# A fused GLA and gated-SSM kernel: the third turn's order, two loads of the second, and the place of an If

## The chip, the cores and the metric

The kernel runs on one core of a Trainium2 chip. The metric is the device time of one execution in microseconds (us). The engines are named as in the profile: PE is TensorE (PEld its weight loads), DVE is VectorE, ACT is ScalarE, POOL is GpSimd, SP is SyncE, which here issues most of the DMAs. Each engine runs its own instructions in the program's order, and engines wait for one another through semaphores.

## The reference

Two layers follow one another. The first is gated linear attention: a state for each of 8 heads decays by alpha and takes in an outer product at each of 768 steps. The second projects the result to a value and a gate, runs a decaying sum over the values, multiplies by the gate's SiLU and projects back. All data are float32 (the weights arrive as float64).

```python
# q, k, v, alpha: (B=4, H=8, S=768, D=48)
for t in range(S):
    state = alpha[:, :, t, :, None] * state + np.einsum('bhd,bhe->bhde', k[:, :, t], v[:, :, t])
    y[:, :, t] = np.einsum('bhd,bhde->bhe', q[:, :, t], state)
x = y.transpose(0, 2, 1, 3).reshape(B, S, H * D)        # (4, 768, 384)
proj = x @ w_in                                         # (4, 768, 1024)
val, gate = proj[..., :512], proj[..., 512:]
a = np.exp(A_log)
for t in range(S):
    h = a * h + val[:, t, :]
    ys[:, t, :] = h
out = (gate * sigmoid(gate) * ys) @ w_out               # (4, 768, 384)
```

## The kernel before

**Two paths.** `fast` computes everything in a way that holds only if the data lie within certain limits (products of alpha not too small, alpha at most 1, weights in a range). While it runs it checks these limits; the result is `flag`, a word that every engine reads (L1122), and `good`, a mask. If the flag is not set, `general` (L19) recomputes everything. It stands in an If (L1136) between `fast` and the last stores. Each engine evaluates that If for itself: it reads the flag into a register and branches. With the inputs here the general path isn't taken, so each engine jumps over its instructions. The last output is copied under the mask `good` (L1142), so that either path's result is the one that is stored (L1143).

**Groups.** The sequence is cut into chunks of 128 steps, two to a group; there are 12 groups (N = 12), three for each batch entry. Attention of a group m needs:

- loads of alpha, keys and queries into `raw_a`, `raw_k`, `raw_q` (`load_raw`, L421; four DMAs each; two buffers of each, taken in turn) and of the values into `v` (`load_v`, L451, two DMAs),
- `products(m)` (L656), a generator. Its steps, each up to a `yield`, are: check of alpha on ACT (`check_alpha`, L623) with a transpose of alpha on DVE (L660), a small product and a memset (L671, L672); the scan of products (L674); reciprocals and the scan of inverses (L695); the transpose of the keys; their product with the inverses (L704); the transpose of the queries; their product (L704). The last four make the tile `Z`, from group 3 on,
- `keys` (PE transposes, L717, and ACT's copy to `ktm`, L718), `scores` (PE, L727), `masks` (ACT's copy of one half and POOL's product with the mask, L742 and L743; DVE's product for the other half, L754), `state` (L786), `values` (L765), `carried` (L776),
- `join` (L791), which copies the result y from PSUM (ACT, L795 to L802) and moves it by eight small DMAs (L812) into `xT`, the layout that the projection needs. Its argument `engines` says which queue issues the moves of the two halves.

**The second layer.** `block(n, cc)` (L845) does a quarter of group n's projection: 12 matmuls (L827) into two PSUM banks, value and gate; DVE's scan `hidden` (L835) reads the value's, ACT's SiLU (L842) the gate's, and POOL multiplies the two to `f` (L843). `output(n)` (L850) multiplies f by `w_out` (16 matmuls, L857), ACT copies (L865) and SP stores (L866). `mm` (L403) hands out three PSUM banks in turn to `keys`, `block` and `output`.

**The order is written out by hand.** `fast` runs in a manual schedule, so each engine gets its instructions in the order of the Python text. The main loop (L1024) has the turns n = 1 to 11; turn n does the second layer of group n, the attention of group m = n + 1, and with `go(k)` the next k steps of `products(n + 2)`. `ahead()` (L1034) issues on SP the loads of group n + 3 and the values of group n + 2. Turns 1 and 2 share a branch of the code (L1040 to L1077); turn n = 2 is the third turn when group 0's, before the loop, is counted. In it DVE, ACT and POOL get `hidden`, `gate` and the masks in the same order as PE its products.

**The end.** `output(N - 1)` multiplies the last group in three pieces (L869 to L878) into the banks b4, b5, b6, after the flag's read and ahead of the If. Behind the If DVE copies each piece under the mask and SP stores it.

Of the kernel before, what the change touches and what calls it, by code (L numbers as in the profile page):

```python
# [10 lines left out]
FP32 = mybir.dt.float32  # L11
# [7 lines left out]
def general(  # L19
# [22 lines left out]
    nc = tc.nc  # L42
    B, H, S, D = q.shape
    DM = H * D
    DI = moe_A_log.shape[0]
    C = 128
    G = 2
    GC = G * C
    NG = S // GC
    NP = H // 2  # L50
    DP = 64
    GP = G * NP
    NK = DM // C
    NI = DI // C
# [8 lines left out]
    const = pool("const", 1)  # L63
    p2 = pool("p2", 2)
    p3 = pool("p3", 3)
# [37 lines left out]
    w_out = const.tile([C, NI, DM], FP32, name="w_out")  # L103
# [34 lines left out]
    for l in LEVELS:  # L138
# [9 lines left out]
        m = const.tile([C, 2 * GP, C // 2], U8, name=f"mask{l}")  # L148
# [21 lines left out]
    def attention(n):  # L170
        nonlocal n_qz
        b, g = divmod(n, NG)
# [1 line left out]
        A = As[n % 2]  # L174


        T = p3.tile([C, 2 * GP * C], FP32, name="T")
        Q = p3.tile([C, G, NP, C], FP32, name="Q")
        K = p3.tile([C, G, NP, C], FP32, name="K")
        aT = T[:, 0:GP * C].rearrange("p (g j t) -> p g j t", g=G, j=NP)  # L180
        for name in "aqk":
            for c in range(G):
# [19 lines left out]
        for l in LEVELS:  # L202
# [10 lines left out]
            for c in range(G):  # L213
                for j in range(NP):
# [5 lines left out]
                    else:  # L220
                        nc.tensor.matmul(sc[:, c, j], K[:, c, j, :], Qz[:, c * NP + j],
                                         start=True, stop=True)
# [26 lines left out]
        for c in range(G):  # L249
# [4 lines left out]
            for h in range(H):  # L254
                nc.tensor.matmul(y[:, h, :], A[:, c, h, :], v_sb[:, c, h, :],
                                 start=(h == 0), stop=(first and h == H - 1), skip_group_check=True)
            if not first:
                for j in range(NP):
                    nc.tensor.matmul(y[:, 2 * j:2 * j + 2, :], Q[:, c, j, :], S_bd[:, j],
                                     start=False, stop=(j == NP - 1), skip_group_check=True)  # L260
# [10 lines left out]
            for j in range(NP):  # L271
                for i in range(2):
                    nc.tensor.matmul(s1[ds(DP * i, DP), j, :], Kn[:, j, i, :], v_sb[:, c, 2 * j + i, :],
                                     start=True, stop=True)
# [56 lines left out]
    for n in range(B * NG + 1):  # L331
# [3 lines left out]
        parts = [attention(n)] if n < B * NG else []  # L335
        parts += [load_weights() if n == 0 else ssm(n - 1)]
        while parts:
            parts = [p for p in parts if next(p, p) is not p]
# [13 lines left out]
def fast(  # L352
# [21 lines left out]
    nc = tc.nc  # L374
    B, H, S, D = q.shape
    DM = H * D
    DI = moe_A_log.shape[0]
    C = 128
    G = 2
# [23 lines left out]
    def mm(*dims, b=None):  # L403
        b = b or next(next_mm)
        return (end_ps if b in "456" else ps).tile([C, *dims], FP32, tag=f"b{b}", name="mm")
# [50 lines left out]


    w_in = [[const.tile([C, NK, C], FP32, name=f"w_in{i}{vg}") for vg in range(2)] for i in range(NI)]
    w_out = const.tile([C, NI, DM], FP32, name="w_out")
    NW = NI + 2  # L460
    bits_in = [[const.tile([C, NK, C, 2], U32, name=f"bits_in{i}{vg}") for vg in range(2)] for i in range(NI)]
    bits_out = const.tile([C, NI, DM, 2], U32, name="bits_out")
# [356 lines left out]

    def project(n, cc):  # L820
        if cc == 0:
            fs[n] = p1.tile([C, NI, GC], FP32, tag="f", name="f")
        xT = xTs[n]
        pv, pg = mm(GC), mm(GC)
        for vg, pj in enumerate((pv, pg)):
            for kk in range(NK):
                nc.tensor.matmul(pj, w_in[cc][vg][:, kk, :], xT[:, kk, :],  # L827
                                 start=(kk == 0), stop=(kk == NK - 1))
        return pv, pg
# [15 lines left out]
    def block(n, cc):  # L845
        pv, pg = project(n, cc)
        hidden(n, cc, pv)
        gate(n, cc, pg)()

    def output(n, banks=(None, None)):  # L850
        b, g = divmod(n, NG)
        if n < N - 1:
            os = [mm(DM, b=b) for b in banks]

        def part(ccs, c):
            for cc in ccs:
                nc.tensor.matmul(os[c], fs[n][:, cc, ds(c * C, C)], w_out[:, cc, :],  # L857
                                 start=(cc == 0), stop=(cc == NI - 1))

        def finish():  # L860
            for c in range(G):
                part(range(split, NI), c)
            for c in range(G):
                o_sb = p3.tile([C, DM], FP32, tag="o_sb", name="o_sb")
                nc.scalar.activation(o_sb, os[c], AF.Copy)  # L865
                nc.sync.dma_start(out=out[b, ds(g * GC + c * C, C), :], in_=o_sb)  # L866

        if n == N - 1:
            pieces = [(0, 0, DM), (1, 0, 2 * C), (1, 2 * C, DM - 2 * C)]  # L869
            os = [end_ps.tile([C, size], FP32, tag=f"b{b}", name="o")  # L870
                  for b, (_, _, size) in zip((4, 5, 6), pieces)]
            for i, ccs in ((0, range(NI - 1)), (1, range(1)), (0, range(NI - 1, NI)), (1, range(1, NI)),
                           (2, range(NI))):
                c, at, size = pieces[i]
                for cc in ccs:
                    nc.tensor.matmul(os[i], fs[n][:, cc, ds(c * C, C)], w_out[:, cc, ds(at, size)],  # L876
                                     start=(cc == 0), stop=(cc == NI - 1))
            return list(zip(pieces, os))  # L878
        split = NI - 1 if n else NI // 2
        for c in range(G):  # L880
            part(range(split), c)
        return finish
# [141 lines left out]
    for n in range(1, N):  # L1024
        m = n + 1
        att = m < N
        steps = products(n + 2) if n + 2 < N else iter(())

        def go(count):
            for _ in range(count):  # L1030
                next(steps, None)


        def ahead():  # L1034
            if n + 3 < N:
                loads(n + 3)
            if n + 2 < N:
                load_v(n + 2, SP)

        if n < 3:  # L1040
            if n == 1:
                block(n, 0)
                for times in [natural_qk(m, name, c, tp) for c in range(G)
                              for name, tp in zip("kq", pair_of(4, C))]:
                    times()
                block(n, 1)
            ahead()
            for c in range(G):
                keys(m, c)
            for c in range(G):  # L1050
                scores(m, c)
            go(1)
            for c in range(G):
                masks(m, c)
            if n == 2:
                block(n, 0)
                go(1)
                block(n, 1)
                go(1)
            else:  # L1060
                block(n, 2)
                go(1)
            state(m, 0)
            values(m, 0)
            values(m, 1)
            state(m, 1)
            carried(m, 0)
            carried(m, 1)
            join(m, (nc.gpsimd, nc.gpsimd) if m == 2 else (SP, SP))
            if n == 2:  # L1070
                go(2)
                block(n, 2)
            go(1)
            block(n, 3)
            go(10)
            output(n)()
            continue  # L1077

        if n == 3:
            for c in range(G):
                scores(m, c, 1 - c)
                masks_apart(m, c)
            for c in range(G):
                keys(m, c)
            ahead()
            go(4)
        else:
            state(n, 0)  # L1090
            values(n, 0)
            values(n, 1)
            state(n, 1)
            carried(n, 0)
            carried(n, 1)
            in_place = join(n, (SP, nc.gpsimd), later=True)
            if att:
                scores(m, 0, 1)
                masks_apart(m, 0)
                in_place()  # L1100
                scores(m, 1, sc=[mm(4, C, b=b) for b in "01"])
                masks_apart(m, 1)
                keys(m, 0, "6")
                keys(m, 1, "4")
            else:
                in_place()
            next_mm = itertools.cycle("160")
            ahead()
            go(4)
            output(n - 1, "50")()  # L1110
        for cc in range(NI):
            block(n, cc)
            go(1)
            if cc == 0 and n == N - 1:
                next(end, None)
            if cc == 2 and n > 3:
                for _ in itertools.islice(checks, 2):
                    pass
        if n == N - 2:
            end = check_end()  # L1120
            next(end)
    value = nc.values_load(flag[0:1, 0:1], min_val=0, max_val=1)  # L1122
    return value, good, output(N - 1)


@with_exitstack
def kernel(ctx: ExitStack, tc: tile.TileContext, *args):
    nc, out = tc.nc, args[-1]
    entries, rows, cols = out.shape
    C = 128  # L1130
    sb = ctx.enter_context(tc.tile_pool(name="end_sb", bufs=1))
    ps = ctx.enter_context(tc.tile_pool(name="end_ps", bufs=1, space=bass.MemoryType.PSUM))
    ends = [sb.tile([C, cols], FP32, name=f"end{c}") for c in range(2)]
    with tc.manual_schedule():
        value, good, os = fast(tc, *args, sb, ps)
    with tc.If(value <= 0):  # L1136
        general(tc, *args, ends)

    with tc.manual_schedule():
        for (c, at, size), o in os:  # L1140
            o_sb = ends[c][:, ds(at, size)]
            nc.vector.copy_predicated(out=o_sb, mask=good.to_broadcast([C, size]), data=o)  # L1142
            nc.sync.dma_start(out=out[entries - 1, ds(rows + (c - 2) * C, C), ds(at, size)], in_=o_sb)  # L1143
# [30 lines left out]
```

## Time and profile before

| | us |
|---|---|
| median of 3 runs | 291.37 (290.88 to 291.85) |
| the profiled execution | 292.39 |
| its span, first to last instruction | 290.7 |
| PE's last matmul ends | 285.7 |
| PE at L827 (projection), 576 matmuls | 127.8 busy |
| PE at L857 (output), 176 matmuls | 59.4 busy |
| DVE at L835 (scans of the second layer), 48 | 34.5 busy |
| ACT busy, whole span | 109.2 |
| DMA, mean rate over the span | 145 GB/s |
| granted TensorE clock, mean | 0.996 |

The profile is of one execution. In rows of 40 slices each digit is the busy share of a 40th of the span (7.27 us) in tenths. A line of a timeline or of the chain begins with the start and the length in us; `[0.67 <-PE mm L827]` behind it is idle time of the engine just before, and what ended it. A group at a line gives the shortest, the median and the longest duration in ns, then the first and the last start in us. In a list of waits the numbers are us in total, times, and longest. A line of DMA issues ends with the median time from issue to landing. A q behind an engine's name marks its sequencer, which waits, branches and issues DMAs.

The granted TensorE clock is full until PE's last matmul. Turns from n = 3 on take about 22 us each; the first 63 us hold the loading and converting of the weights and turns 0 and the most of 1.

### The profile page before, as it was taken

What the parts mean: (1) busy time and instruction counts of PE and PEld (TensorE: products, weight loads), DVE (VectorE), ACT (ScalarE), POOL (GpSimd) and SP (SyncE); (2) the same over time, 40 slices, a digit from 0 to 9 for tenths busy, and PEclk for the clock granted to TensorE, in tenths of its full rate; (3) what the DMA queues carried; (4) which work ended last, traced back from release to release, by engine and by line L of the source; (5) the groups of instructions that cost most, each with busy time, mean ns of one, the idle gap of its engine ahead of it and who ended that gap; (6) DMA issues with size and microseconds to landing.
All of it is one profiled execution on the core that took longest, in us unless ns stands there. A gap on an engine that the chain in (4) does not pass through costs nothing.

```text
span 290.7 us, 6236 instructions
## 1 busy us (share of the span) xinstructions
PE 279.0 (96%) x2353; PEld 226.8 (78%) x2353; DVE 211.3 (73%) x263; ACT 109.2 (38%) x242; POOL 139.2 (48%) x165
## 2 busy tenths in 40 slices
PE   6699999999999999999999999999999999999993
PEld 6578877885886988788788788788788788787872
DVE  5998887999899999399499499499599590140221
ACT  3357634433341626226326316316316316212210
POOL 7138791375532765526625625626725725523120
PEclk9999999999999999999999999999999999999998
DMA  9999969999997893992991991991991401101101
GB/s 131 163 169 284 373 128 184 174 252 214 209 217 123 214 201 63 227 189 66 227 175 43 213 206 43 222 199 44 214 207 44 108 2 41 57 0 43 55 3 62
DMA packets 70734, 42.08 MB, mean 145 GB/s; under 512 B 47508, under 2 KB 69656, under 8 KB 70696
## 3 DMA queue, kind: packets, MB, share of 16 engines
q1 hardware_dynamic: 68240, 39.78, 69.6%
q0 software_dynamic: 1408, 1.62, 2.3%
q8 instruction: 20, 0.33, 0.5%
q10 hardware_dynamic: 1048, 0.20, 0.4%
q14 instruction: 18, 0.15, 0.2%
HBM read 33.33 MB, written 4.72 MB: 131 GB/s over the span
## 4 chain that ended last, share of the span: by engine, by line
PE 81%; DVE 9%; DMA 4%; issue 2%; SPq 1%; ACT 1%; POOL 0%; DVEq 0%; ACTq 0%; POOLq 0%
PE mm L827 38%; PE mm L857 18%; PE pair L765 6%; PE pair L727 5%; PE st L786 3%; PE pair L776 3%; PE mm L717 3%; PE mm L727 2%; DMA raw_q<-in_q_dram 2%; PE o L876 2%; DMA raw_k<-in_k_dram 2%; DVE prod L674 2%; SPq L445 1%; PE pair L605 1%; DVE pair L552 1%
## 5 line engine op out<-in xcount | busy, mean ns | idle before, releaser
L827 PE MATMUL mm<-xT,w_in 128*128 128x256 f32 x576 | 127.8, 380 | 0.4 <-ACT A L742 0.4
L827 PEld LDWEIGHTS mm<-xT,w_in 128*128 128x128 f32 x576 | 108.7, 190 | 17.8 <-issue 0.6
L843 POOL TENSOR_TENSOR f<-sg,hh 128x256 f32<-128x256 f32 x48 | 40.4, 843 | 87.7 <-ACT sg L842 62.8
L835 DVE TENSOR_TENSOR_SCAN hh<-a_dec,hh,mm 128x256 f32<-128x256 f32 x32 | 23.7, 741 | 49.8 <-PE mm L827 45.0
L857 PE MATMUL mm<-w_out,f 128*128 128x384 f32 x176 | 59.4, 488 | 0.1
L842 ACT ACTIVATE sg<-mm 128x256 f32<-128x256 f32 x48 | 18.4, 384 | 97.4 <-PE mm L827 95.3
L750 POOL TENSOR_TENSOR A<-A,mask 128x512 f32<-128x512 f32 x32 | 47.7, 1521 | 5.5 <-ACT A L749 5.4
L857 PEld LDWEIGHTS mm<-w_out,f 128*128 128x128 f32 x176 | 32.5, 190 | 21.2 <-POOL f L843 0.7
L812 POOL DMA_DIRECT2D xT<-y_sb x44 | 22.7, 521 | 28.5 <-ACT y_sb L796 26.8
L674 DVE TENSOR_TENSOR_SCAN prod<-aT,first 128x1024 f32<-128x1024 f32 x10 | 23.4, 2338 | 0.3
L695 DVE TENSOR_TENSOR_SCAN inv<-aT,last 128x1025 f32<-128x1025 f32 x10 | 22.9, 2294 | 0.3
L765 PE MATMUL pair<-A,v 128*64 128x128 f32 x352 | 21.3, 274 | 0.0
L865 ACT ACTIVATE o_sb<-mm 128x384 f32<-128x384 f32 x22 | 10.8, 491 | 25.5 <-PE mm L857 25.2
L727 PE MATMUL pair<-Z 48*128 48x128 f32 x272 | 18.9, 282 | 0.5 <-DVE Z L704 0.3
L765 PEld LDWEIGHTS pair<-A,v 128*64 128x64 f32 x352 | 19.1, 137 | 0.0
L727 PEld LDWEIGHTS pair<-Z 48*128 48x128 f32 x272 | 16.3, 187 | 3.3 <-issue 2.2
L743 POOL TENSOR_TENSOR A<-A,mask 128x512 f32<-128x512 f32 x8 | 10.1, 1273 | 17.7 <-ACT A L742 17.7
L660 DVE STREAM_TRANSPOSE Z<-raw_k 128x1024 f32<-128x1024 f32 x9 | 18.5, 2053 | 0.0
L660 DVE STREAM_TRANSPOSE aT<-raw_a 128x1024 f32<-128x1024 f32 x9 | 18.4, 2044 | 0.0
L660 DVE STREAM_TRANSPOSE Z<-raw_q 128x1024 f32<-128x1024 f32 x9 | 18.2, 2023 | 0.0
L835 DVE TENSOR_TENSOR_SCAN hh<-a_dec,mm 128x256 f32<-128x256 f32 x16 | 10.8, 675 | 8.6 <-PE mm L827 7.0
L786 PEld LDWEIGHTS st<-v,ktm 128*64 128x64 f32 x320 | 11.4, 137 | 3.5 <-issue 3.5
(128 smaller groups left out, 299.6 us busy)
## 6 DMA issues: line engine op xcount, KB each, us to landing
raw_k<-in_k_dram SPq DMA_DIRECT2D x24, 192.0 KB, 5.3
raw_q<-in_q_dram SPq DMA_DIRECT2D x24, 192.0 KB, 6.5
v<-in_v_dram SPq DMA_DIRECT2D x24, 192.0 KB, 7.2
raw_a<-in_alpha_dram SPq DMA_DIRECT2D x23, 192.0 KB, 4.0
out_dram<-o_sb SPq DMA_DIRECT2D x22, 192.0 KB, 3.9
raw_a<-in_alpha_dram SPq DMA_DIRECT2D x18, 176.0 KB, 4.1
raw_k<-in_k_dram SPq DMA_DIRECT2D x18, 176.0 KB, 5.3
raw_q<-in_q_dram SPq DMA_DIRECT2D x18, 176.0 KB, 6.9
```

The lines of the kernel that those rows point to most:

```text
L660: nc.vector.transpose(out=to.rearrange("p h (c j) -> p h j c", j=NT), in_=raw_bufs[m % NR][name].rearrange("p h (j d) -> p h j d", d=D)[:, ...
L674: nc.vector.tensor_tensor_scan(out=prod, data0=al, data1=first.rearrange("p h n -> p (h n)"), initial=0.0, op0=ALU.mult, op1=ALU.max)
L695: nc.vector.tensor_tensor_scan(out=inv[:, ::-1], data0=aT[:, ::-1], data1=lasts[:, 0:4 * GC + 1][:, ::-1], initial=0.0, op0=ALU.mult, op1= ...
L727: nc.tensor.matmul(sc[i][:, p, :], Z[rows, p, 1, cols], Z[rows, p, 0, cols], start=True, stop=True)
L750: nc.gpsimd.tensor_mul(A[:, i], A[:, i], mask_all())
L765: nc.tensor.matmul(ys[m][i][ds(64 * s, 64), e, ds(c * C, C)], v_sb[:, c, 2 * p + i, :], A[:, i, p, :], start=(c == 0 and e == 0), stop=Fal ...
L786: nc.tensor.matmul(st[ds(64 * i, 64), p, :], ktms[c][:, p, i, :], vs[m % NV][:, c, 2 * p + i, 0:D], start=(ch == 0 and p == 0), stop=(ch = ...
L812: engines[s].dma_start(out=xT[ds(row, size), kk], in_=y_sb[ds(64 * s + d, size), a])
L827: nc.tensor.matmul(pj, w_in[cc][vg][:, kk, :], xT[:, kk, :], start=(kk == 0), stop=(kk == NK - 1))
L835: nc.vector.tensor_tensor_scan(out=hh, data0=a_dec[:, cc:cc + 1].to_broadcast([C, GC]), data1=pv, initial=prev_h[cc][:, GC - 1:GC] if n % ...
L843: return lambda: nc.gpsimd.tensor_mul(fs[n][:, cc, :], sg, hhs.pop((n, cc)))
L857: nc.tensor.matmul(os[c], fs[n][:, cc, ds(c * C, C)], w_out[:, cc, :], start=(cc == 0), stop=(cc == NI - 1))
```

## The change

Four things are edited.

1. In turn n = 1 only alpha of group 4 is loaded ahead of `keys`. The keys and queries of group 4 and the values of group 3 are loaded by SP behind `join(2)`. The moves of `join(2)` are issued half by SP and half by POOL, instead of all by POOL.
2. Turn n = 2 starts (behind its loads) with `block(2, 0)`, ahead of `keys(3)`; `block(2, 1)` and `block(2, 2)` stand behind the masks, each with one step of `products(4)`, and only `block(2, 3)` stands behind `join(3)`. One step of products, not two, stands ahead of the last blocks.
3. `output(N - 1)` no longer computes the last product. `fast` returns `f` and `w_out`, and the three pieces are multiplied behind the If, in the same order and into the same banks. In the program, each engine's choice of path now stands ahead of the last product.
4. So that `f` and `w_out` outlive `fast`, they move to the pool `end_sb`; in `general`, T, Q and K get two buffers instead of three.

```diff
@@ general
-        T = p3.tile([C, 2 * GP * C], FP32, name="T")
-        Q = p3.tile([C, G, NP, C], FP32, name="Q")
-        K = p3.tile([C, G, NP, C], FP32, name="K")
+        T = p2.tile([C, 2 * GP * C], FP32, name="T")
+        Q = p2.tile([C, G, NP, C], FP32, name="Q")
+        K = p2.tile([C, G, NP, C], FP32, name="K")
@@ fast
-    w_out = const.tile([C, NI, DM], FP32, name="w_out")
+    w_out = end_sb.tile([C, NI, DM], FP32, name="w_out")
...
-            fs[n] = p1.tile([C, NI, GC], FP32, tag="f", name="f")
+            fs[n] = end_sb.tile([C, NI, GC], FP32, tag="f", name="f")
...
-            ahead()
+                load_raw("a", n + 3, [SP])
+            else:
+                ahead()
+                block(n, 0)
             for c in range(G):
                 keys(m, c)
...
             for c in range(G):
                 masks(m, c)
             if n == 2:
-                block(n, 0)
-                go(1)
                 block(n, 1)
                 go(1)
-            else:
-                block(n, 2)
-                go(1)
+            block(n, 2)
+            go(1)
             state(m, 0)
...
-            join(m, (nc.gpsimd, nc.gpsimd) if m == 2 else (SP, SP))
-            if n == 2:
-                go(2)
-                block(n, 2)
+            join(m, (SP, nc.gpsimd) if m == 2 else (SP, SP))
+            if n == 1:
+                for name in "kq":
+                    load_raw(name, n + 3, [SP])
+                load_v(n + 2, SP)
             go(1)
             block(n, 3)
             go(10)
...
-    return value, good, output(N - 1)
+    return value, good, fs[N - 1], w_out
@@ tile_gla_recurrent__then__mamba_gated_ssm_out_kernel
-        value, good, os = fast(tc, *args, sb, ps)
+        value, good, f, w_out = fast(tc, *args, sb, ps)
     with tc.If(value <= 0):
         general(tc, *args, ends)
 
     with tc.manual_schedule():
-        for (c, at, size), o in os:
+        pieces = [(0, 0, cols), (1, 0, 2 * C), (1, 2 * C, cols - 2 * C)]
+        os = [ps.tile([C, size], FP32, tag=f"b{b}", name="o") for b, (_, _, size) in zip((4, 5, 6), pieces)]
+        parts = f.shape[1]
+        for i, ccs in ((0, range(parts - 1)), (1, range(1)), (0, range(parts - 1, parts)),
+                       (1, range(1, parts)), (2, range(parts))):
+            c, at, size = pieces[i]
+            for cc in ccs:
+                nc.tensor.matmul(os[i], f[:, cc, ds(c * C, C)], w_out[:, cc, ds(at, size)],
+                                 start=(cc == 0), stop=(cc == parts - 1))
+        for (c, at, size), o in zip(pieces, os):
             o_sb = ends[c][:, ds(at, size)]
             nc.vector.copy_predicated(out=o_sb, mask=good.to_broadcast([C, size]), data=o)
```

The piece of `output` that computed the last product (L868 to L878), with its condition at L852, is removed.

More of the change, by code (lines that the diff above doesn't have):

```diff
@@ L851, in output @@
         b, g = divmod(n, NG)
-        if n < N - 1:
-            os = [mm(DM, b=b) for b in banks]
+        os = [mm(DM, b=b) for b in banks]
         def part(ccs, c):
@@ L866, in finish @@
                 nc.sync.dma_start(out=out[b, ds(g * GC + c * C, C), :], in_=o_sb)
[L868 to L878, printed above, removed]
         split = NI - 1 if n else NI // 2
```

## The prediction

> **What bounds the kernel now.** I read the page first, then the chain of waits, then single stretches. All times are microseconds from the start of the profiled execution.
>
> ```profile
> span 290.7 us, 6236 instructions
> PE 279.0 (96%) x2353; PEld 226.8 (78%) x2353; DVE 211.3 (73%) x263; ACT 109.2 (38%) x242; POOL 139.2 (48%) x165
> DVE  5998887999899999399499499499599590140221
> ```
>
> PE is busy nearly throughout, so only two things can pay: PE's few stops, and the time after its last matmul. The reader should also see DVE's row of nines from slice 6 to slice 14 (about 45 to 107): there DVE is as full as PE.
>
> The chain of waits in the stretch that the change touches:
>
> ```profile
> 65.68 5.54 PE L857 MATMUL mm<-w_out,f 128*128 128x384 f32 x16
> 72.24 0.14 issue
> 72.38 1.59 PE pair L727 x24
> 73.97 0.50 ACT A L742
> 74.47 0.32 issue
> 74.79 5.56 PE mm L827 x24
> 94.29 1.99 PE pair L727 x32
> 96.27 1.02 PE mm L717 x8
> 97.30 0.87 PE mm L827 x4
> ```
>
> (The first line is PE's timeline, the rest the chain.) Sums from this chain: 12 matmuls of a block cost 2.59 in the steady turns (10.36 for 48), an output product 5.16. From 62.98 to 97.30 PE does five blocks (12.95), two outputs (10.34), the smaller products of two groups (9.4): 32.7 of work in 34.3. So 1.6 is lost: about 0.2 in the output at 65.68 (5.38 to the next line's start, against 5.16), 0.3 before and 0.4 within the scores at 72.38, 0.3 in the two blocks at 74.79, the rest in crumbs. The two waits have plain causes: the scores wait for DVE's product at 71.00 (1.23 long), and block(2,0) for moves of y that POOL issued at 64.0 to 67.5 and that landed 7.2 to 8.2 later, up to 75.7, behind loads that SP had queued.
>
> DVE one turn later:
>
> ```profile
> 99.27 0.62 DVE L835 TENSOR_TENSOR_SCAN hh<-a_dec,mm 128x256 f32<-128x256 f32 x1
> 99.81 2.25 DVE L704 TENSOR_TENSOR Z<-Z,inv 128x1024 f32<-128x1024 f32 x1
> 101.98 0.67 DVE L835 TENSOR_TENSOR_SCAN hh<-a_dec,mm 128x256 f32<-128x256 f32 x1
> ```
>
> A block takes two of three PSUM banks in rotation, so the gate half of block(3,1), due on PE at 97.30+2.59+1.30=101.2, needs the bank that the scan at 99.27 reads until 99.89; that of block(3,2), due at 103.8, the one read until 102.65. DVE is thus only 1.1 to 1.3 ahead of PE. That is the room for any gain before it.
>
> The end, from the groups at the If's line, the waits of SP and the DMA issues:
>
> ```profile
> L1136 DVEq COMPARE_BRANCH  x1: 72/72/72, 280.0 to 280.0; - x1
> L1136 PEldq COMPARE_BRANCH  x1: 3878/3878/3878, 282.3 to 282.3; - x1
> L1136 DVEq EVENT_SEMAPHORE  x1: 21/21/21, 283.1 to 283.1; - x1
> L1136 PEldq EVENT_SEMAPHORE  x1: 51/51/51, 286.3 to 286.3; - x1
> SPq L1169 <- DMA out_dram<-end: 2.5, 1, 2.5
> out_dram<-end SPq DMA_DIRECT2D x1, 128.0 KB, 1.7
> out_dram<-end SPq DMA_DIRECT2D x1, 64.0 KB, 3.6
> ```
>
> The smallest store takes longest. Narrow windows of the DMA view say why: its packets run from 286.9 to 287.3, one 16 KB instruction packet from 287.6 to 288.5, then nine packets of the store, until 289.0.[...] That queue (20 packets of 16 KB) fits PE, which has most of the instructions, and the fetch comes 1.4 after PE passes the If at 286.25.
>
> [...] DVE's next instruction comes 3.1 after its branch, ACT's and POOL's 2.7.[...] PE reads the flag at 277.55, while matmuls enough to 280.49 are still to run.[...] DVE's product is 2.25 at 99.81, under POOL's mask products (96.09 to 103.16), and 1.22 at 84.65.
>
> **The change part by part.**
>
> *Pools and tiles.* The general path's three tags go from three buffers to two, and f and w_out move to the outer pool. That path isn't taken; no executed instruction is added: 0.
>
> *Moves of y and loads in turn n=1.* SP issues raw_a of group 4 (59.60 to 62.2) as before. Then come four moves by SP and four by POOL instead of eight by POOL, at 64.0 to about 66.5, and behind them SP's 8 key and query issues and 2 for v: at 0.31 to 0.43 each[...], 66.5 to about 71. The last DMA ahead of the moves lands at 67.45;[...] they land by about 68.6 rather than 75.7. The loads end no later than before (DMA is full either way, about 77 for v, used at about 81.6 now; keys of group 4 at 84.2). POOL ends its moves 2.05 earlier, so f(1,3) is ready by 68 rather than 69.6 and the output ends at 65.68+5.18=70.86 (-0.2).
>
> *Block(2,0) first.* PE: block 70.86, keys 73.45, scores 74.47, block(2,1) 76.46, block(2,2) 79.05, states and values 81.64, block(2,3) 85.02, output 87.6, scores of group 4 at 92.8 instead of 94.29: -1.5, if nothing is late. What is late next is DVE. Its first scan waits for block(2,0): 72.26 to 72.95; transpose, product and memset (2.35) to 75.3; the first mask needs scores at 74.47+1.1: 75.6 to 76.2. The second mask follows ACT's copy of its scores, and ACT is now late as well: keys' copies to 75.25, check_alpha 1.15+0.20, two copies of 0.6 to 77.4, where before they ended at 75.1. So the mask ends at 78.1. DVE has been idle some 1.6, against 0.67 before. Of the work behind it, one scan fewer remains: 90.03-76.51-0.64=12.9 gives 91.0, and block(2,3)'s scan at 86.42, the turn of the keys now ahead of it, costs a little more: 91.2 to 91.4 instead of 90.03. DVE is 1.2 to 1.3 later where its room was 1.1 to 1.3. Hence block(3,1) gets its bank at 99.89+1.3=101.2, block(3,2) at 102.65+1.3=103.95 (due 103.8). PE's 1.5 is taken back: between 0 and +0.25. If POOL's masks, which start 1.4 earlier, free the 2.25 product of some of its excess, 0 to -0.3. I take +0.1, bounds -0.5 and +0.6.
>
> *Group 3's moves of y* follow carried at 85.0; SP is then stopped[...] until about 90, as at 85.61 now (first issue 4.49 long), so they land at about 95.7 as now, and block(3,0) at 95.7 needs the last only 0.9 into its matmuls. Cost 0; with the DMA 1 later about 0.5, and that would only spend what DVE takes anyway.
>
> *The choice ahead of the last product.* PE's flag read is at 277.55, its branch at about 278.1. Bounds for its next instruction: it also waits for PE's own last matmul at 280.5, so no sooner than 280.6; no later than branch + 3.88 = 282.0, unless the branch holds the fetch back. With DVE's 3.1[...]: 281.4. A weight load and its lead add 0.35, so the product starts at 281.7 instead of 280.35 to 280.5: +1.2 (bounds +0.4, +2.1). All four f are there (281.8 for the last, first used 2.4 into the product). In return PE's second fetch falls at about 282.8, ahead of all stores. The 64 KB store then lands after its last data packet, 1.2 from its issue, plus the 0.36 that the 128 KB one shows: 1.55 instead of 3.57, -2.0. Sum -0.8, bounds -1.6 and +0.1. The other engines' branches stay.
>
> Sum: +0.1-0.8=-0.7. The profiled execution took 292.39, 1.7 outside its span; the median shown is 291.37. Nothing outside the span is touched, so I put the difference on the median: 290.7.
>
> **The rivals.** *A, as summed:* 290.7, its own range 290.0 to 291.5. *B, DVE keeps its lead:* mask products and copies overlap better, POOL's earlier masks free DVE, and 1.2 of PE's 1.5 stays. For it: POOL's masks stretch DVE by a full 1.0 at 99.81. Against: ACT's check_alpha sits between the keys and the second mask. -1.2-0.8=-2.0: 289.4. *C, slower: PE holds the branch until its array has drained and fetches only then.* For it: PE's branch alone shows 3878 ns, ending 0.45 after the last matmul. Against: an instruction packet starts at 283.83, before that drain. Price: 280.5+3.1+0.35=283.95, +3.5-2.0+0.1=+1.6: 293.0. It decides once PE stands over 2 us. *D, the store gains nothing,* because another fetch or a slow DMA engine strikes it again: +1.2+0.1=+1.3: 292.7. For it: ACT and POOL fetch late too (second packets at 284.7 and 284.9). Against: those come before the stores of a later product.
>
> **How the numbers follow.** A 0.50, B 0.20, C 0.15, D 0.15. About 0.3%, 0.87 us, is what a measurement of this kernel can tell from no change. A's spread reaches past -0.87: 0.18 faster, 0.31 same, 0.01 slower. B is faster 0.19, same 0.01; C slower 0.13, same 0.02; D slower 0.12, same 0.03. Together 0.37, 0.37, 0.26. The range 289.3 to 292.8 takes in B and D and leaves out most of C.
>
> **What would show it.** Moves of group 2's y landing near 69, block(2,0) at about 70.9 with no stop at the scores; PE about 1.4 ahead at 93 and stopped for DVE's scans in blocks (3,1) and (3,2), level again at 107; a hole of about 1.2 on PE before the last product; the last store at about 1.6. Wrong would be: PE still ahead at 107 (B), a hole over 2 (C), a last store over 3 (D), or block(2,0) waiting for moves.

## The result: slower, and the profile after

| | before | after |
|---|---|---|
| median, us | 291.61 (290.88 to 291.99, 4 runs) | 296.02 (294.66 to 296.75, 4 runs) |
| ratio, 95% interval | | 1.0141 [1.0112, 1.0170] |
| the profiled execution, its span | 292.39, 290.7 | 295.32, 293.5 |

The medians differ by 4.4 us (by themselves they give a ratio of 1.0151; the table has the ratio and interval on record). 290.7 was predicted. The two profiled executions are not at their medians: that of before took 0.8 more, that of after 0.7 less, so their spans show only 2.8 of the 4.4. The page of after begins so:

```profile
span 293.5 us, 6235 instructions
PE 281.3 (96%) x2353; PEld 229.0 (78%) x2353; DVE 212.6 (72%) x263; ACT 108.8 (37%) x242; POOL 137.3 (47%) x161
...
L827 PE MATMUL mm<-xT,w_in 128*128 128x256 f32 x576 | 128.1, 380 | 3.5 <-DVE hh L835 3.5
```

PE does the same 2353 matmuls. What is new is the idle time at the end of the projection's row: 3.5 us, all of it waiting for `hh`, DVE's scan of the second layer (L835). PE's timeline (start, length) tells where:

```profile
71.73 2.75 PE L827 MATMUL mm<-xT,w_in 128*128 128x256 f32 x12
74.33 1.04 PE L717 MATMUL mm<-ident,Z 128*128 128x128 f32 x8
75.29 2.06 PE L727 MATMUL pair<-Z 48*128 48x128 f32 x32
...
94.00 2.06 PE L727 MATMUL pair<-Z 48*128 48x128 f32 x32
...
96.92 4.05 PE L827 MATMUL mm<-xT,w_in 128*128 128x256 f32 x18
104.45 6.74 PE L827 MATMUL mm<-xT,w_in 128*128 128x256 f32 x30 [3.48 <-DVE hh L835]
```

Before, PE went through the four blocks of group 3 without a stop:

```profile
94.22 2.06 PE L727 MATMUL pair<-Z 48*128 48x128 f32 x32
...
97.13 10.53 PE L827 MATMUL mm<-xT,w_in 128*128 128x256 f32 x48
```

At 63.9, ahead of all that the change touches in PE's order, this execution was 0.9 later than that of before. Its TensorE clock was at half (0.50 granted) from 14.0 to 17.4, where that of before has 1.00; that this made all of the 0.9 isn't shown (the profile of the order alone, further down, is 0.8 late at the same point with full clock there: its mean of 0.989 over 299.9 us is used up by the two stretches of 3.4 at half clock listed at the end). I take the 0.9 off as this execution's own. Then the first five lines are what was forecast: block(2,0) begins at 71.73 straight behind the output, nothing stops at the scores, and the scores of group 4 begin at 94.00, or 93.1 without the 0.9, against 94.22 before. PE had won 1.1 against this profile of before. The last line takes it back three times over: PE wanted the bank for the gate half of block(3,1) at 100.97 and got it at 104.45. The states of that turn begin at 111.12 instead of 107.59, 3.53 later, or 2.6 without the 0.9, and all later turns keep these 3.53.

DVE's timeline shows why the bank came so late:

```profile
73.31 0.75 DVE L835 TENSOR_TENSOR_SCAN hh<-a_dec,hh,mm 128x256 f32<-128x256 f32 x1 [0.54 <-PE mm L827]
...
78.25 0.69 DVE L754 TENSOR_TENSOR A<-pair,mask 128x512 f32<-128x512 f32 x1 [1.08 <-ACT A L742]
...
79.54 2.85 DVE L674 TENSOR_TENSOR_SCAN prod<-aT,first 128x1024 f32<-128x1024 f32 x1
...
83.33 2.83 DVE L695 TENSOR_TENSOR_SCAN inv<-aT,last 128x1025 f32<-128x1025 f32 x1
...
97.57 1.05 DVE L681 TENSOR_TENSOR ratio<-prod,last 128x4 f32<-128x4 f32 x1
...
98.87 3.11 DVE L695 TENSOR_TENSOR_SCAN inv<-aT,last 128x1025 f32<-128x1025 f32 x1
101.90 2.02 DVE L660 STREAM_TRANSPOSE Z<-raw_k 128x1024 f32<-128x1024 f32 x1
103.78 0.61 DVE L835 TENSOR_TENSOR_SCAN hh<-a_dec,mm 128x256 f32<-128x256 f32 x1
104.32 1.19 DVE L704 TENSOR_TENSOR Z<-Z,inv 128x1024 f32<-128x1024 f32 x1
```

And the same operations before:

```profile
77.17 2.27 DVE L674 TENSOR_TENSOR_SCAN prod<-aT,first 128x1024 f32<-128x1024 f32 x1
...
80.38 2.29 DVE L695 TENSOR_TENSOR_SCAN inv<-aT,last 128x1025 f32<-128x1025 f32 x1
...
94.74 0.17 DVE L681 TENSOR_TENSOR ratio<-prod,last 128x4 f32<-128x4 f32 x1
...
95.15 2.29 DVE L695 TENSOR_TENSOR_SCAN inv<-aT,last 128x1025 f32<-128x1025 f32 x1
```

From the product of group 3's queries (71.00 before, 71.54 after) to the scan that frees the bank (99.27 and 103.78) DVE does the same instructions in 28.27 and in 32.24, 3.97 more. The lines add up to it: waits 0.54 + 1.08 where there were 0.67 (+0.95); the two scans of turn 2 2.85 + 2.83 where there were 2.27 + 2.29 (+1.12); the small product and the inverse scan of turn 3 1.05 + 3.11 where there were 0.17 + 2.29 (+1.70); 0.2 in crumbs. The stretched operations lie beside POOL's:

```profile
77.74 2.50 POOL L743 TENSOR_TENSOR A<-A,mask 128x512 f32<-128x512 f32 x2 [1.90 <-ACT A L742]
80.69 2.21 POOL L843 TENSOR_TENSOR f<-sg,hh 128x256 f32<-128x256 f32 x1 [0.45 <-ACT sg L842]
83.28 0.73 POOL L843 TENSOR_TENSOR f<-sg,hh 128x256 f32<-128x256 f32 x1 [0.38 <-ACT sg L842]
...
95.87 8.41 POOL L750 TENSOR_TENSOR A<-A,mask 128x512 f32<-128x512 f32 x4 [5.54 <-ACT A L749]
```

The same masks before:

```profile
96.09 7.11 POOL L750 TENSOR_TENSOR A<-A,mask 128x512 f32<-128x512 f32 x4 [5.38 <-ACT A L749]
```

In turn 3 POOL's masks start at 95.87 (96.09 before, so 1.1 earlier without the 0.9), while DVE comes to its small product 2.83 later (1.9 without the 0.9). Before, the one operation stretched under them was the product of 2.25, which stands *behind* the scan that frees the bank. Now they lie over the small product and the inverse scan ahead of that scan, and the product is back at 1.19.

The end of after, from the groups at the If's line, the timeline and the waits of SP:

```profile
L1125 PEldq COMPARE_BRANCH  x1: 3329/3329/3329, 281.7 to 281.7; - x1
```

```profile
283.89 0.81 PE L1136 MATMUL o<-w_out,f 128*128 128x384 f32 x2
...
285.18 4.79 PE L1136 MATMUL o<-w_out,f 128*128 128x384 f32 x22 [0.48 <-PEq L1125]
...
290.00 0.30 DVE L1140 COPY_PREDICATED end<-good,o 128x128 f32<-128x128 uint8 x1 [0.45 <-PE o L1136]
```

```profile
SPq L1167 <- DMA out_dram<-end: 0.8, 2, 0.5
SPq L1167 <- PEq L1167: 0.7, 2, 0.5
```

PE's branch lasts until 285.0. Two of the 24 records of the last product, its first matmul, stand ahead of the hole. They ran from 283.89, while the branch was still under way, although the text has all twelve behind the If. The last copy starts at 290.00; before it was 285.75, and PE is 3.53 later, so the hole costs 290.00 - 285.75 - 3.53 = 0.72. SP's wait for the last stores went from 2.5 to 0.8, and from the last copy to the end of the span it takes 3.5 instead of 4.95, 1.45 less. In these two profiles the end thus gains 1.45 - 0.72, about 0.7. The experiments show that the 1.45 is the sum of two edits: the If's move gains 1.88 there, and the edit of loads and moves loses 0.4.

### The profile page after: what moved, and what is told of

It reads as the page before. It is cut to its first block, busy times and chain, and to the rows that moved or that the text cites. A ratio compares the mean times of both kernels' runs of the same rounds, so it can differ in the third digit from the quotient of the medians.

```text
span 293.5 us, 6235 instructions
## 1 busy us (share of the span) xinstructions
PE 281.3 (96%) x2353; PEld 229.0 (78%) x2353; DVE 212.6 (72%) x263; ACT 108.8 (37%) x242; POOL 137.3 (47%) x161
## 5 line engine op out<-in xcount | busy, mean ns | idle before, releaser
L843 POOL TENSOR_TENSOR f<-sg,hh 128x256 f32<-128x256 f32 x48 | 39.3, 818 | 94.6 <-ACT sg L842 69.5
L835 DVE TENSOR_TENSOR_SCAN hh<-a_dec,hh,mm 128x256 f32<-128x256 f32 x32 | 23.7, 741 | 49.6 <-PE mm L827 44.9
L842 ACT ACTIVATE sg<-mm 128x256 f32<-128x256 f32 x48 | 18.5, 385 | 102.4 <-PE mm L827 94.3
L750 POOL TENSOR_TENSOR A<-A,mask 128x512 f32<-128x512 f32 x32 | 48.9, 1558 | 5.7 <-ACT A L749 5.5
L812 POOL DMA_DIRECT2D xT<-y_sb x40 | 20.7, 522 | 28.1 <-ACT y_sb L796 26.5
L695 DVE TENSOR_TENSOR_SCAN inv<-aT,last 128x1025 f32<-128x1025 f32 x10 | 24.3, 2429 | 0.3
L674 DVE TENSOR_TENSOR_SCAN prod<-aT,first 128x1024 f32<-128x1024 f32 x10 | 24.0, 2397 | 0.3
L743 POOL TENSOR_TENSOR A<-A,mask 128x512 f32<-128x512 f32 x8 | 10.1, 1276 | 16.3 <-ACT A L742 11.7
L835 DVE TENSOR_TENSOR_SCAN hh<-a_dec,mm 128x256 f32<-128x256 f32 x16 | 10.8, 674 | 8.7 <-PE mm L827 7.1
```

What stands on the lines that cost most here:

```text
L674: nc.vector.tensor_tensor_scan(out=prod, data0=al, data1=first.rearrange("p h n -> p (h n)"), initial=0.0, op0=ALU.mult, op1=ALU.max)
L695: nc.vector.tensor_tensor_scan(out=inv[:, ::-1], data0=aT[:, ::-1], data1=lasts[:, 0:4 * GC + 1][:, ::-1], initial=0.0, op0=ALU.mult, op1= ...
L750: nc.gpsimd.tensor_mul(A[:, i], A[:, i], mask_all())
L812: engines[s].dma_start(out=xT[ds(row, size), kk], in_=y_sb[ds(64 * s + d, size), a])
L835: nc.vector.tensor_tensor_scan(out=hh, data0=a_dec[:, cc:cc + 1].to_broadcast([C, GC]), data1=pv, initial=prev_h[cc][:, GC - 1:GC] if n % ...
L842: nc.scalar.activation(sg, pg, AF.Silu)
```

## The experiments

Every ratio is against the kernel before on the same chip (medians 291.76, 291.56 and 291.58 in the three batches), with its 95% interval. The differences in us are between medians.

### The change in its parts

**The end alone.** The last product behind the If, f and w_out in `end_sb`, the general path's tags in two buffers; the turns as before.

```diff
-    return value, good, output(N - 1)
+    return value, good, fs[N - 1], w_out
...
-        for (c, at, size), o in os:
+        for i, ccs in ((0, range(parts - 1)), (1, range(1)), (0, range(parts - 1, parts)),
+                       (1, range(1, parts)), (2, range(parts))):
...
```

> Edits 3 and 4 (the last product behind the If, f and w_out in the outer pool) with the turns of before. Theory T: no stop at 101; a hole of 1.3 us on PE before the last product, the last store landing in 1.6 instead of 3.6 us: about -0.7 us. Rival R: +1.5 to +4 us, and the start (to 45 us) about 1 us later.

Measured: 290.99, ratio 0.9975 [0.9966, 0.9984], 0.77 faster. Its last two stores, in the profile's DMA issues:

```profile
out_dram<-end SPq DMA_DIRECT2D x1, 128.0 KB, 1.7
out_dram<-end SPq DMA_DIRECT2D x1, 64.0 KB, 1.5
```

The last store lands 1.5 after its issue (3.6 before). From the last copy to the end of the span it takes 288.9 - 285.83 = 3.07, where before took 4.95: 1.88 less. So this half gained what the forecast said, and the loss comes with edits 1 and 2. This is the lowest median on record, below both kernels.

The turns in it are those of before, so its profile is a second look at them:

```profile
74.20 5.50 PE L827 MATMUL mm<-xT,w_in 128*128 128x256 f32 x24
...
93.57 2.06 PE L727 MATMUL pair<-Z 48*128 48x128 f32 x32
```

Here block(2,0) doesn't stop: the moves of y land 6.8 to 7.8 after their issue instead of 7.2 to 8.2. From the start of block(1,3) to the scores of group 4 PE takes 30.74 (93.57 - 62.83), in the profile of before 31.24 (94.22 - 62.98). Half a us of what the change was to win was that one execution's own. After takes 30.12 (94.00 - 63.88), so against this profile PE's lead is only 0.62.

**The turns alone**, and each of their two edits alone. The first diff is the loads and moves, the second the order.

```diff
-            ahead()
+            if n == 1:
+                load_raw("a", n + 3, [SP])
+            else:
+                ahead()
...
-            join(m, (nc.gpsimd, nc.gpsimd) if m == 2 else (SP, SP))
+            join(m, (SP, nc.gpsimd) if m == 2 else (SP, SP))
+            if n == 1:
+                for name in "kq":
+                    load_raw(name, n + 3, [SP])
+                load_v(n + 2, SP)
```

```diff
             ahead()
+            if n == 2:
+                block(n, 0)
...
             if n == 2:
-                block(n, 0)
-                go(1)
                 block(n, 1)
                 go(1)
-            else:
-                block(n, 2)
-                go(1)
+            block(n, 2)
+            go(1)
...
-            if n == 2:
-                go(2)
-                block(n, 2)
             go(1)
             block(n, 3)
```

Both:

> Edits 1 and 2 (loads and moves of turn 1, order of turn 2) on the kernel before; the last product stays ahead of the If, f and w_out in their old pools. Theory T (the order makes DVE late, POOL's products slow DVE further, PE stops in block(3,1)): the stop of 3.5 us at about 101 comes again, +2.6 us or more. Rival R (the moved tiles or the If behind the flag cost the time in most runs): about -0.3 to +0.5 us.

Measured: 297.50, ratio 1.0185 [1.0165, 1.0205], +5.7. Order alone:

> Edit 2 alone (block(2,0) ahead of the keys), loads and moves as before. Theory T: block(2,0) waits for moves that land at 75.7, so PE stops about 4 us at 71, DVE's masks and products of group 4 come later still and block(3,1) waits again: +5 us or more. Rival R2: about +0.5 us.

Measured: 301.80, ratio 1.0354 [1.0330, 1.0377], +10.0. Loads alone:

> Edit 1 alone (alpha of group 4 ahead, its keys and queries and the values of group 3 behind the moves, moves half on SP and half on POOL), order of turn 2 as before. Theory T: moves land near 69, block(2,0) no longer waits, DVE's idle 0.67 at 75.8 shrinks: -0.5 to -1.0 us. Rival R2 (it is the later loads that hurt): +1 us or more.

Measured: 291.76, ratio 1.0003 [0.9992, 1.0015], no change, so the expected gain is missed. The loads with the end's move:

> Edits 1, 3 and 4, with the order of turn 2 as before. If the gain of the If (-0.75 us) stands alone: -0.75 us against before. If the 0.9 us by which PE was ahead in the one profile of the loads alone reaches the end as well: -1.2 to -1.6 us.

Measured: 291.33, ratio 0.9988 [0.9979, 0.9998], no better than the end alone (the intervals overlap).

The order is what costs. Without the earlier moves, it costs more, as PE's timeline of that kernel shows:

```profile
75.11 4.35 PE L827 MATMUL mm<-xT,w_in 128*128 128x256 f32 x12 [3.11 <-DMA xT<-y_sb]
...
109.44 2.93 PE L827 MATMUL mm<-xT,w_in 128*128 128x256 f32 x6 [3.50 <-DVE hh L835]
```

Block(2,0) waits 3.11 for the moves of y, then the same stop as in after follows. So the loads' edit is needed for the new order, and by itself brings nothing: in its profile the moves land early and PE reaches the scores of group 4 at 93.32 instead of 94.22, but the medians are equal. Of that 0.9, half is the late profile of before (93.57 in that of the end alone). The other half is given back at the very end. SP's waits behind the last stores are these in the end alone, without the loads' edit,

```profile
SPq L1166 <- DMA out_dram<-end: 0.5, 1, 0.5
SPq L1166 <- PEq L1166: 0.4, 1, 0.4
```

and these in the loads with the end's move:

```profile
SPq L1173 <- DMA out_dram<-end: 0.8, 2, 0.5
SPq L1173 <- PEq L1173: 0.7, 2, 0.5
```

The profile counts two waits for the stores and two for PE's queue instead of one of each, and from the last copy to the end it takes 3.53 instead of 3.07. All seven profiles with both edits, after's among them, take 3.45 to 3.53. With the last product ahead of the If the loads' edit costs the same there: 5.34 against 4.95. Why there is one wait more is not shown.

One thing more is in the first line: 12 matmuls took 4.35 instead of 2.75. In the kernel with both edits the 30 matmuls behind the stop took 9.46 instead of the 6.74 of after. A table of windows of that kernel has the granted clock (PEclk) in it:

```profile
core 0: us, PE busy (x) PEld busy (x) DVE busy (x) ACT busy (x) POOL busy (x), PEclk, DMA share, GB/s
95.00:102.30 7.30, 5.15 (x32) 4.22 (x28) 7.20 (x5) 3.93 (x8) 7.24 (x4) 1.00 0.89 215
102.40:109.20 6.80, 5.55 (x13) 4.48 (x14) 4.84 (x5) 0.38 (x1) 3.32 (x3) 0.50 1.17 201
```

Behind the stop of 3.50 TensorE ran at half clock for 6.8 us in this execution. That is a second cost of the same stop: 9.46 - 6.74 = 2.7 us here, 1.6 for the first stop of the order alone (4.35 instead of 2.75, clock at half for 3.4). The profiled execution of after, with its stop of 3.48, kept the full clock there (1.00 from 95 to 116).

### What the stop is made of

**POOL's masks over DVE in turn 3.** In after, POOL's mask products of group 4 are left out, so that its attention is unmasked there.

```diff
-            nc.gpsimd.tensor_mul(A[:, i], A[:, i], mask_all())
+            if m != 4:
+                nc.gpsimd.tensor_mul(A[:, i], A[:, i], mask_all())
```

> The changed kernel with POOL's four mask products of group 4 left out (its scores stay unmasked, so the values of group 4 are others). Theory P (POOL's products hold up DVE's in turn 3): DVE's small product at L681 takes 0.2 instead of 1.05 and the inverse scan 2.3 instead of 3.1, the stop shrinks from 3.5 to about 1.8, no half clock: +0.3 to +1.2 us against before. Rival (DVE is late from turn 2 alone): stop and time as in the changed kernel, +4.4 us.

Measured: 293.19, ratio 1.0049 [1.0033, 1.0066], +1.6 where after has +4.4. DVE and PE of it:

```profile
97.42 0.17 DVE L681 TENSOR_TENSOR ratio<-prod,last 128x4 f32<-128x4 f32 x1
...
97.83 2.29 DVE L695 TENSOR_TENSOR_SCAN inv<-aT,last 128x1025 f32<-128x1025 f32 x1
```

```profile
102.57 6.74 PE L828 MATMUL mm<-xT,w_in 128*128 128x256 f32 x30 [1.75 <-DVE hh L836]
```

Both operations have their old lengths and the stop is halved, by 1.73: just the 1.70 of the sum above. The mean clock is 1.0. What is left, 1.75, is near what the forecast's own sum gives for a stop: DVE 1.3 later, PE 1.4 earlier, room 1.2, so 1.5.

**POOL's f products over DVE in turn 2.** In after, the products for f in block(2,1) and block(2,2) are left out; f is ACT's SiLU alone there. Then with the masks of group 4 left out as well.

```diff
+        if n == 2 and cc in (1, 2):
+            nc.scalar.activation(fs[n][:, cc, :], pg, AF.Silu)
+            hhs.pop((n, cc))
+            return lambda: None
         nc.scalar.activation(sg, pg, AF.Silu)
```

> The changed kernel with POOL's products for f in blocks (2,1) and (2,2) left out (ACT writes the SiLU to f, so half of group 2's f is not multiplied by the scan). Theory P: DVE's two scans for group 4 at about 80 and 83 take 2.3 each instead of 2.85, DVE is 1.1 us earlier, the stop shrinks to about 2.4, clock full: +1.3 to +2.3 us against before. Rival (no hold-up by POOL there): +4.4 us.

> Both left out, POOL's products for f in blocks (2,1) and (2,2) and its masks of group 4. If the two add up: stop about 0.7 us, time about level with before (-0.7 to +0.3 us). If one makes the other void: as the better of the two alone.

Measured: 296.56, 1.0158 [1.0130, 1.0187], and 292.90, 1.0041 [1.0026, 1.0056]: the same as after and as the kernel without the masks. A miss. The first one's DVE timeline says why:

```profile
78.97 2.84 DVE L674 TENSOR_TENSOR_SCAN prod<-aT,first 128x1024 f32<-128x1024 f32 x1
...
82.75 2.29 DVE L695 TENSOR_TENSOR_SCAN inv<-aT,last 128x1025 f32<-128x1025 f32 x1
...
87.08 0.75 DVE L835 TENSOR_TENSOR_SCAN hh<-a_dec,hh,mm 128x256 f32<-128x256 f32 x1
```

L695 is back at 2.29, so the f products did stretch it; but L674 stays at 2.84 (in after it starts at 79.54, under POOL's masks of group 3, which run from 77.74 to 80.24). And the 0.54 won is hardly kept: the next scan, of block(2,3), comes 0.28 earlier against the start of the stretch (87.08 - 70.95 here, 87.95 - 71.54 in after), for now it has PE's matmuls to wait for. The stop is 3.28 instead of 3.48. With the masks of group 4 left out as well it is 1.57 instead of 1.75.

**ACT's check ahead of the second mask.** In after, `check_alpha(4)` stands behind the masks, so that ACT's copy for DVE's second mask comes earlier.

```diff
         if m >= NAT:
-            check_alpha(m)
+            if m != 4:
+                check_alpha(m)
...
             if n == 2:
+                check_alpha(4)
                 block(n, 1)
```

> The changed kernel with check_alpha(4) on ACT behind the masks of group 3 instead of ahead of them. Theory A (ACT, late with the keys, holds DVE's second mask): DVE's idle 1.08 before that mask goes, everything on DVE comes about 1 us sooner, the stop shrinks to about 2.4 and the clock stays full: +1.3 to +2.3 us against before. Rival: DVE waits elsewhere instead, +4.4 us.

Measured: 295.76, ratio 1.0131 [1.0109, 1.0154], no change from after. Another miss, from its DVE timeline:

```profile
77.05 0.69 DVE L755 TENSOR_TENSOR A<-pair,mask 128x512 f32<-128x512 f32 x1 [0.92 <-ACT A L743]
...
78.50 2.31 DVE L675 TENSOR_TENSOR_SCAN prod<-aT,first 128x1024 f32<-128x1024 f32 x1
...
86.61 0.75 DVE L836 TENSOR_TENSOR_SCAN hh<-a_dec,hh,mm 128x256 f32<-128x256 f32 x1 [0.63 <-PE mm L828]
```

The check was hardly what DVE waited for: 0.92 is left of 1.08. With the check out of the way, ACT's copy for that mask waits 0.27 for PE's scores instead. The scans of turn 2 happen to be short here, and again it is of no use, since DVE then waits 0.63 for PE. Turn 3 is as in after, stop 3.27.

### What the half clock is worth

In after, seven spare matmuls of the block's shape are put into bank b4 ahead of the gate half of block(3,1), where PE would stand.

```diff
         for vg, pj in enumerate((pv, pg)):
+            if (n, cc, vg) == (3, 1, 1):
+                spare = mm(GC, b="4")
+                for _ in range(7):
+                    nc.tensor.matmul(spare, w_in[cc][0][:, 0, :], xT[:, 0, :], start=True, stop=True)
```

> The changed kernel with seven spare matmuls (3 us of PE work into a free PSUM bank, read by nobody) ahead of the gate half of block(3,1), where PE stops for 3.5 us. Theory H (a stop[...] halves TensorE's clock[...], and that is the part of the loss that the stop alone does not give): no stop over 0.6 us, clock full over 100 to 112, +2.0 to +3.0 us against before in place of +4.4. Rival (the clock plays no part): +4.4 us as the changed kernel.

Measured: 294.77, ratio 1.0104 [1.0086, 1.0123], +3.2. PE's timeline:

```profile
99.77 3.19 PE L829 MATMUL mm<-xT,w_in 128*128 128x256 f32 x14
103.43 6.74 PE L831 MATMUL mm<-xT,w_in 128*128 128x256 f32 x30 [0.48 <-DVE hh L839]
```

The spare work fills the hole. From the start of block(3,0) to the matmul behind the hole PE takes as long as in after (95.88 to 103.43 here, 96.92 to 104.45 there), and yet the time is +3.2 instead of +4.4. The mean clock was at least 0.998 in all of its runs; in after's it was 1.0 in the run of 294.66 and 0.994 in the other three. The run of after with full clock thus agrees with the filled one. The intervals of the two ratios just overlap, so the 1.2 for the half clock is an estimate. That half clock goes with a long stop is better shown by the mean clocks of all executions: with a stop of 3.27 or more in the profile and the If moved (after, f of turn 2 left out, check behind the masks) 12 of 14 have 0.994 or less, with a stop of at most 1.75 (the filled kernel and the two without the masks of group 4) all 29 have 0.997 or more. Where in an execution the clock was low is seen in the profiled ones alone.

## Why the prediction was wrong

**The step that failed** is the last part of "Block(2,0) first": "PE's 1.5 is taken back: between 0 and +0.25 ... If POOL's masks, which start 1.4 earlier, free the 2.25 product of some of its excess, 0 to -0.3. I take +0.1, bounds -0.5 and +0.6." The term stands for the edits of the turns. Measured it is about +4.0 at full clock (3.2 of the filled kernel and the 0.77 that the If gains in it), and +5.2 as the medians stand, with a low mean clock in three of after's four executions (4.4 + 0.77; the turns alone gave 5.7). Of the 4.0, 3.1 lie on PE in turns 2 and 3: from block(1,3) to group 3's output it takes 53.55 in after (117.43 - 63.88) and 50.42 in the end alone (113.25 - 62.83). They are the stop of 3.48, less the lead of 0.62, and 0.3 in crumbs. 0.4 lie at the very end, in SP's waits. The last 0.5 I can't place. In its parts:

- *DVE's waits in turn 2:* forecast 1.6 against 0.67. Measured 0.54 + 1.08 = 1.62. The size is right, but not the cause given for the second: leaving ACT's check out of its way is worth only 0.16.
- *POOL over DVE in turn 3:* forecast as a gain of up to 0.3, measured as 1.70 of loss, and shown by leaving the masks out. The forecast saw that masks of POOL stretch a DVE operation, saw that their place against DVE's order would shift, and let them free an operation without asking which one they would lie on instead. The masks did come 1.1 earlier, but DVE, by the forecast's own sum, 1.3 later: both move them onto operations that stand earlier in DVE's order. The forecast had the figures for it: masks at 96.09 - 1.4 = 94.7, the small product at 94.74 + 1.3 = 96.0, so the product would start under them. The traces show both cases: before, the inverse scan that started at 95.15, ahead of the masks at 96.09, kept its 2.29; in after, with the masks ahead at 95.87, a 128x4 product of 0.17 took 1.05 at 97.57 and the scan took 3.11 at 98.87. The product and the scan were longer where the masks had started first, and they stood ahead of the release. Why they are longer there is not shown.
- *POOL over DVE in turn 2:* not in the forecast; +1.12. It matters less than its size, as the tries that took part of it away show: DVE then waits for PE at the last scan of the turn.
- *The room.* "DVE is 1.2 to 1.3 later where its room was 1.1 to 1.3" was the right frame, and foresaw a stop. With 3.97 of lateness in it, and 0.54 of the start, the bank comes at 99.89 + 4.51 = 104.40, and PE went on at 104.45.
- *The clock:* not in the forecast. In the profiled executions the two stops of the order alone (3.11 and 3.50) were each followed by half clock for 3.4 us, that of the order and loads (3.50) by half clock for 6.8, and the 3.48 of after was not, nor was the 0.48 of the filled kernel. Without the masks of group 4 (stops of 1.75 and 1.57) the mean clock was 1.0. So the length of the stop doesn't decide alone.

**What held.** *The moves of y:* forecast to land by 68.6; they landed 1.9 to 2.2 after issues of 64.6 to 66.5, that is by 68.7 with the 0.9 in it, and block(2,0) didn't wait. *PE's lead:* 92.8 forecast for the scores of group 4, 93.1 measured; but the 1.5 was reckoned from stops of one execution, and against the other profile of the same turns 0.62 is left of it. *The choice ahead of the product:* -0.8 forecast, -0.77 measured alone. That it fits so well is in part luck. PE resumes where it was forecast (281.7; measured 285.18 - 3.53 = 281.65), but one matmul of the product ran from 283.89, ahead of the branch's end at 285.0, and the hole costs 0.72, not 1.2. The last store lands at 1.5 in the end alone, as forecast (1.55); after's profile has no landing of it. That gives 1.88 where 2.0 was forecast. That the instruction packet delayed the store of before was the author's estimate; only the order of the packets is shown. The two make -1.16 in the profiles, but the medians show -0.77: the store of before doesn't always land as late as 3.6 (2.8 in the profile of the order alone, whose end is that of before).

**The rivals.** Of the four cases none held. C and D put the danger at the end, where the hole stayed under 2 and the store came early. B, that DVE keeps its lead, was furthest off. The case for slower should have been put where the forecast itself had found no room: there 1.70 more of DVE cost PE 1.73.

## What to carry to other kernels

When work is moved on one engine, list for every pair of engines that contend (here DVE and POOL: 0.17 became 1.05) what will lie beside what afterwards, and price the operation that is newly covered, not only the one that is freed; what counts is whether it stands ahead of or behind the instruction that releases the bottleneck. Where an engine has 1 us of room ahead of the bottleneck, a change that wins 1.5 us on the bottleneck upstream can't keep it, and in this kernel a delay of 1.70 beyond the room was paid in full. Before a wait is counted as a gain, look at it in a second execution: here 0.5 of the lead was not there in it. Of the four stops of 3.1 to 3.5 us on TensorE whose clock is read place by place in the last section, three were charged twice, by the wait and by half clock after it.

## What was not expected of the hardware

- Behind a stop TensorE ran at half clock for 3.4 us twice and for 6.8 once. The first 3.4 cost 1.6 for 12 matmuls of 128x256 (4.35 instead of 2.75), the 6.8 cost 2.7 for 30 (9.46 instead of 6.74).
- The profiled executions, with the granted clock by stretches of the timeline, or where none was taken the mean of the execution:

| kernel | stop | granted clock |
|---|---|---|
| order alone, first stop | 3.11 | 0.97 from 71 to 75, 0.50 to 78, 0.98 to 82 |
| order alone, second stop | 3.50 | 0.99 from 105 to 109, 0.50 to 112.3, 1.00 to 116 |
| order and loads | 3.50 | 1.00 from 95 to 102.3, 0.50 from 102.4 to 109.2, 1.00 to 116 |
| after | 3.48 | 1.00 from 95 to 102.3 and from 102.4 to 116 |
| filled | 0.48 | 1.00 from 95 to 110 |
| check behind the masks | 3.27 | mean 0.994 |
| f of turn 2 left out | 3.28 | mean 0.994 |
| masks of group 4 left out | 1.75 | mean 1.0 |

  After's 3.48 is the only one of the four long stops with a clock by stretches that has no half clock behind it. A mean of 0.994 over 294 us is 3.5 us at half clock (an estimate: 0.006 * 294 * 2), but the mean doesn't say where: after's own 0.994 is the half clock from 14.0 to 17.4. What brought that one, and what spared after's stop, is not shown.
- A 128x4 product on DVE took 1.05 (at 97.57 in after) instead of 0.17 under POOL's mask products (95.87 to 104.28), six times as long, while the STREAM_TRANSPOSE beside them (101.90) kept its 2.02.
- In after PE's branch lasted 3.33, while those of the other engines lasted 0.05 to 0.07; on these the wait shows as the gap to their next instruction instead (DVE's branch at 283.5, next at 286.4).
